# One core, a chunked linear-attention scan and a routed MLP: the loads around the triangular inverses put in another order

## The chip, the cores and the metric

The kernel runs on one core of one Trainium2 chip. A core has five engines that run their own instruction queues side by side: TensorE (PE, with weight loads shown apart as PEld), VectorE (DVE), ScalarE (ACT), GpSimd (POOL) and SyncE (SP). SP computes nothing here; it issues most of the transfers (DMAs), one after the other, and each transfer is carried by the same 16 DMA engines. Every engine takes its instructions strictly in the order in which the program lists them, so an instruction that waits holds up all that is behind it on the same engine. The metric is the device time of the whole kernel in microseconds, the median of some runs.

## What is computed

The reference has two parts. The first is a recurrence over 768 time steps for 4 batches of 8 heads with 40 channels each:

```python
for t in range(S):
    y[:, :, t] = np.einsum('bhd,bhde->bhe', rt, state)
    Sa = np.einsum('bhde,bhe->bhd', state, at)
    state_decay = state * wt[:, :, None, :] - np.einsum('bhd,bhe->bhde', Sa, bt)
    state = state_decay + np.einsum('bhd,bhe->bhde', vt, kt)
```

The second part takes the 3072 rows of y (320 wide) as tokens of a mixture of 8 experts. Each token goes to the expert with the largest logit; an expert keeps the 80 tokens with the largest gate weight and drops the others; each kept token runs through `relu(x @ w1[e]) @ w2[e]` times its gate weight, and every other row of the output is zero.

## The kernel before

**Chunks and units.** The recurrence is cut into 12 chunks of 64 steps. A unit `n` is one chunk of one pair of batches, so there are 24 units (`NU`), and the main loop runs n = 0 to 25. Within a chunk the dependence of the steps on each other is a triangular system for each head. It is solved with inverses of its 32 x 32 diagonal blocks. The blocks of four units (`NG = 4`) are inverted together, one block on each of the 128 partitions, so there are six inversions k = 0 to 5, and inversion k serves units 4k to 4k+3.

**The state's loop.** Unit n needs the state that unit n-2 leaves (two pairs of batches take turns). The path goes: `summed` writes the state on DVE (line 528), POOL copies it (`own_apart`, line 223), PE multiplies it in (`right`, line 447), ACT copies the sum, PE applies the first diagonal inverses (`diagonal(n, 0)`, line 460), then `below` (line 471), then `diagonal(n, 1)`, and `summed(o)` of the unit before, o = n-1, ends the unit with 32 products (line 525). In the same unit the decays and the system of a unit eight ahead, m = n+8, and the scaled keys of m+1 are made (`inverted`, line 326, on DVE, from the keys and b's in `raw_s`; `operand` turns them on PE, line 247).

**The inversion's round trip.** An inversion goes through memory twice:

- `system_kept(m)` writes a unit's blocks to the DRAM tensor `blocks` (line 353).
- `fetch(k)` reads the blocks of four units into the tile `lt` (line 365; 4 transfers of 128 KB, on SP). `lt` and `tt` have one buffer each.
- `begin(k)` masks `lt` into `tt` on POOL (line 370).
- `step(k, i)`, i = 1 to 30, are two DVE instructions each (lines 381 and 384) that work on `lt` and `tt`.
- `end(k)` writes `tt` to `solved` (line 387), and `returned(k)` reads it back into `dt` in another layout (line 394; 4 transfers of 128 KB), from where `diagonal` takes it.

**The order of the work.** The order on each engine is written out by hand: `do(f)` chains the instructions of each call behind the ones before, engine by engine. So the order of calls in the loop is the order of every queue, SP's included. Inversion k = n/4 + 1 begins in the unit with n % 4 = 0 (called the opening unit below: n = 0, 4, 8, 12, 16), and its 30 steps are spread over that unit and the three that follow. `pause(steps, us)` takes steps from the list until their estimated costs use up `us`; with 100 it takes all that are left. Once the list is empty, `end` is called, and `returned` a little later.

In the fourth unit of a group the calls that matter here stand in this order: the last steps, `end`, `load(m + 2, "s")` (keys and b's, 4 transfers of 80 KB), `returned` (4), `turned_r` with the load of the next r (2), `fetch` of the next inversion (4), and after these, in `summed` and in the next unit, the loads of v, w and a (2 each) and the unit's own `blocks` (2). All are on SP from the middle of the prelude on (`queues[1] = nc.sync`).

**Lists and experts.** While the last units run, and after them, DVE finds the 80 best gate values per expert by rounds of `max` and `match_replace` (lines 577 and 578), then the kept tokens' numbers are counted out: a threshold is put on all partitions by PE (line 956), two products give counts and positions (lines 966 and 969), a scan and some DVE work give each token's slot, and 24 products with one-hot tiles `hot` (line 985) give the lists of token numbers. `keep_at_work(pool, tag, times)` issues `times` products of zeros of 128 x 256 in bf16 on PE (line 143), whose result nobody reads. Then the experts' rows are gathered and multiplied.

Of the kernel before, what the change touches and what calls it, by code (L numbers as in the profile page):

```python
# [18 lines left out]
def kernel(  # L19
# [42 lines left out]
    NG = 4  # L62
    NCI = NM // NG
# [73 lines left out]
    still = const.tile([128, 256], BF16, name="still")  # L137
    nc.vector.memset(still, 0.0)

    def keep_at_work(pool, tag, times, x=still):  # L140
        p = pool.tile([128, 256], F32, name="still_p", tag=tag)
        for _ in range(times):
            nc.tensor.matmul(p, lhsT=x[:, 0:128], rhs=x, start=True, stop=True)


    with ExitStack() as p1:

        AHEAD = 2 * NG
        NU = NM
# [540 lines left out]
        def do(f, *args):  # L690
            traced = nc.cur_bb.bb.instructions
            at = len(traced)
            f(*args)
            traced = nc.cur_bb.bb.instructions
            for i in traced[at:]:
                if i.engine in kinds:
                    if i.engine in latest:
                        tc.add_manual_dep(i, latest[i.engine], mybir.DependencyInfo(
                            mybir.DependencyClass.NoSync, mybir.DependencyReason.DATA), reason="order")
                    latest[i.engine] = i.name  # L700


        steps, rounds_ = [], []

        def pause(todo, us_):
            while todo and us_ > 0:
                cost, f = todo.pop(0)
                do(f)
                us_ -= cost

        def invert(k):
            steps.extend(((i * (C - 1 - i) * 1.04 + 155) * 2e-3, lambda i=i: step(k, i)) for i in range(1, C - 1))
# [53 lines left out]
        do(operand, NG + 4, False)  # L766
        do(fetch, 1)

        waiting, turn, inverting = [], None, None

        ZEROS = NU - N // zrows
# [2 lines left out]
        for n in range(NU + 2):  # L774
            o, m = n - 1, n + AHEAD
            now, past, coming, next_, begins_ = n < NU, 0 <= o < NU, m < NU, m + 1 < NU, n % NG == 0


            small = []
            if waiting and (n % NG == 0 or not coming):  # L780
                turn, small, then = waiting.pop(0)
            if next_:
                do(decays, m + 1)
            if n == NU - 2:
                do(turned_lists)
            if past:
                do(turned, o)
            if n == NU - 2:
                do(rows_of_lists)
                rounds_.extend(merged)  # L790
            if coming:
                do(system, m)
            if next_:
                do(forward, m + 1)
                do(backward, m + 1)
            pause(small, 1 if coming else 100)
            if next_:
                do(turned_a, m + 1)
            do(together, n, o)
            if past:  # L800
                do(kept_state, o)
            if now:
                do(right, n)
            if coming:
                do(system_kept, m)
            if next_:
                do(doubled, m + 1)
            if now:
                do(right_kept, n)
            if past:  # L810
                do(state_kept, o)
            if begins_ and n + NG < NU:
                inverting = n // NG + 1
                do(begin, inverting)
            pause(steps, 0.7)
            if next_:
                do(decayed_a, m + 1)
            pause(small, 1)
            if begins_ and inverting:
                invert(inverting)  # L820
            pause(steps, 1.6 if begins_ else 0.4)
            if n == NU:
                pause(rounds_, 2)
            back = None
            if inverting and not steps:
                do(end, inverting)
                back, inverting = inverting, None
            if past:
                do(lower, o)
            if coming:  # L830
                do(psi_masked, m)
            if turn and not coming:
                do(turn)
                rounds_.extend(then)
                turn = None

            if next_ and not begins_:
                do(inverted, m + 1)
            if now and begins_:
                do(reads_g, n)  # L840
            if now:
                do(diagonal, n, 0)
            if now and not begins_:
                do(reads_g, n)
            if begins_ and o >= 1:
                do(logits, o - 1)
            if now:
                do(below, n)
            if next_ and begins_:
                do(inverted, m + 1)  # L850
            pause(steps, (2.4, 4.4, 4.4, 100)[n % NG] if coming else (4.5, 6.5, 100, 100)[n % NG])
            pause(rounds_, LISTS.get(n, 0))
            if inverting and not steps:
                do(end, inverting)
                back, inverting = inverting, None
            if next_:
                do(load, m + 2, "s")
            if back:
                do(returned, back)
            if n == NU + 1:  # L860
                do(keep_at_work, ps_t, "t", 14)
            if o >= 1 and not begins_:
                do(logits, o - 1)
            if turn:
                do(turn)
                turn = None
            if now:
                do(turned_r, n)
            if n % NG == NG - 1 and n + 1 + NG < NU:
                do(fetch, (n + 1) // NG + 1)  # L870
            if now:
                do(reads_r, n)
                do(diagonal, n, 1)
                do(beside, n)
            if next_:
                do(operand, m + 1)
            if n == NU:
                do(keep_at_work, ps_t, "t", 12)
            if past:
                do(summed, o)  # L880
            if n == NU:
                do(keep_at_work, ps_t, "t", 10)
            if o >= 1:
                do(rows_out, o - 1)
                do(logits_summed, o - 1)
                i = share_of[o - 1]
                if o - 1 == shares[i][-1]:
                    waiting.append(gate(i))
            if 0 <= n - ZEROS < N // zrows:
                do(fill, n - ZEROS, n)  # L890
# [51 lines left out]
    with ExitStack() as p2:  # L942
        sl = p2.enter_context(tc.tile_pool(name="sl", bufs=1))
        ps_l = p2.enter_context(tc.tile_pool(name="ps_l", bufs=1, space=PSUM))

        keep_at_work(ps_l, "still", 56)
        union = sl.tile([E, cap], F32, name="union")
        nc.vector.tensor_tensor(out=union, in0=lists[0][0:E, 0:cap], in1=lists[1][0:E, 0:cap][:, ::-1], op=Alu.max)  # L950
        thr = sl.tile([E, 1], F32, name="thr")
# [15 lines left out]

        pos = ps_l.tile([128, NSEL], F32, name="pos")
        nc.tensor.matmul(pos, lhsT=behind_b, rhs=selm, start=True, stop=True)
        at = sl.tile([128, NSEL], F32, name="at")  # L970
        nc.vector.tensor_tensor_scan(at, seg, tot, 0.0, op0=Alu.mult, op1=Alu.add)
        nc.vector.scalar_tensor_tensor(out=at, in0=at, scalar=1.0, in1=pos, op0=Alu.add, op1=Alu.add)
# [127 lines left out]
```

## Time and profile before

| what | us |
|---|---|
| median of 3 runs | 600.25 (597.84 to 607.77) |
| the profiled execution, its own time | 595.1 |
| its span, first to last instruction | 593.4 |
| PE busy in the span | 474.4 (80%) |
| DVE busy in the span | 384.1 (65%) |
| ACT, POOL busy | 219.0, 186.8 |
| mean granted TensorE clock | 0.889 |

The profile is of one execution. Busy shares are means over stages of different kinds: the recurrence fills the span up to about 478 us, the lists lie between about 478 and 511 us, the experts after that. For each instruction the trace has its start, its duration, the idle time of its engine before it and what ended that idle time. The granted clock is the share of full speed that TensorE's throttle allows.

### The profile page before, as it was taken

How to read it: one execution, taken by the hardware profiler on the slowest of the kernel's cores; microseconds unless marked ns; L12 is line 12 of the kernel's file. 1: busy time of each engine (PE TensorE's matmuls, PEld its weight loads, DVE VectorE, ACT ScalarE, POOL GpSimd, SP SyncE). 2: the span in 40 equal slices, each digit the busy share in tenths (PEclk: the TensorE clock that was granted, in tenths of full speed). 3: DMA queues.
4: the chain of work that ended last, by engine and by line, in shares of the span. 5: the costliest groups of instructions: out<-in, count | busy, mean ns of one | idle time of the engine just before them, and what ended most of it. 6: DMA issues, size and time to landing. Idle time of an engine off the chain costs nothing. (4 is left out here: it accounts for less than half of the span.)

```text
span 593.4 us, 25360 instructions
## 1 busy us (share of the span) xinstructions
PE 474.4 (80%) x11254; PEld 404.6 (68%) x11254; DVE 384.1 (65%) x871; ACT 219.0 (37%) x416; POOL 186.8 (31%) x277
## 2 busy tenths in 40 slices
PE   3876328599949999599968998698989835999996
PEld 2665317488848888488857887587878724877774
DVE  8766972699738994699748973988468988001010
ACT  1332114265534565266543655254545300010100
POOL 5243111234534442444532444142323210311011
PEclk9977558599968999699987999698999967999999
DMA  4679438554665548565575437236533239899100
GB/s 78 117 148 136 79 86 130 94 109 76 133 103 104 104 89 156 99 108 102 116 125 99 79 91 111 65 71 138 103 72 92 59 96 359 282 372 362 43 15 14
DMA packets 245249, 71.45 MB, mean 120 GB/s; under 512 B 229524, under 2 KB 237972, under 8 KB 245140
## 3 DMA queue, kind: packets, MB, share of 16 engines
q1 hardware_dynamic: 215136, 61.80, 47.6%
q10 hardware_dynamic: 29236, 6.41, 5.7%
q8 instruction: 88, 1.44, 1.0%
q0 software_dynamic: 768, 1.64, 0.9%
q14 instruction: 21, 0.17, 0.1%
HBM read 51.69 MB, written 18.12 MB: 118 GB/s over the span
## 5 line engine op out<-in xcount | busy, mean ns | idle before, releaser
L381 DVE TENSOR_TENSOR tmp<-tt,lt 128x30 f32<-128x30 f32 (+9 forms) x180 | 75.1, 417 | 45.6 <-POOL tt L370 41.1
L384 DVE TENSOR_TENSOR tt<-tt,tmp 128x30 f32<-128x30 f32 (+9 forms) x180 | 88.8, 493 | 6.6
L265 POOL TENSOR_SCALAR_AFFINE_SELECT side<-side 64x1024 f32<-64x1024 f32 x46 | 53.0, 1152 | 48.5 <-ACT side L511 47.0
L247 PE MATMUL tp<-ident,scaled 64*128 64x64 f32 x384 | 21.8, 262 | 40.7 <-DVE scaled L326 37.8
L223 POOL COPY apart<-state 64x320 f32<-64x320 f32 x44 | 20.1, 457 | 107.4 <-DVE state L528 102.0
L525 PE MATMUL yp<-side,scaled 128*64 128x128 f32 (+1 forms) x768 | 50.8, 290 | 2.5 <-POOL side L265 1.9
L1053 DVE TENSOR_SCALAR y<-yp,weight 80x320 f32<-80x320 f32 x8 | 4.4, 547 | 70.1 <-PE yp L1051 70.1
L265 POOL TENSOR_SCALAR_AFFINE_SELECT nt<-nt 64x512 f32<-64x512 f32 x48 | 32.4, 674 | 55.0 <-ACT nt L350 52.7
L247 PEld LDWEIGHTS tp<-ident,scaled 64*128 64x128 f32 x384 | 17.6, 167 | 44.4 <-issue 30.7
L525 PEld LDWEIGHTS yp<-side,scaled 128*64 128x64 f32 x768 | 44.8, 148 | 4.4 <-POOL side L265 2.0
L291 DVE TENSOR_TENSOR_SCAN pt<-decay,begins 128x520 f32<-128x520 f32 x24 | 34.5, 1437 | 13.7 <-ACT decay L285 12.4
L350 ACT COPY nt<-sp 128x1024 f32<-128x1024 f32 x24 | 24.3, 1011 | 47.4 <-DVE ends L296 29.5
L1045 ACT ACTIVATE hT<-hp 128x320 f32<-128x320 f32 x16 | 6.1, 434 | 92.5 <-PE hp L1041 92.5
L460 PE MATMUL pr<-yy,dt 32*32 32x40 f32 x1536 | 37.6, 200 | 0.1
L1051 PE MATMUL yp<-w,hT 128*80 128x320 f32 x128 | 37.4, 439 | 0.0
L418 PE MATMUL yp<-rT,gT 64*64 64x64 f32 x768 | 28.6, 225 | 10.1 <-DVE xT L534 8.6
L312 POOL COPY qd<-qt 128x1024 f32<-128x1024 f32 x24 | 25.0, 1042 | 36.2 <-DVE qt L298 26.5
L460 PEld LDWEIGHTS pr<-yy,dt 32*32 32x32 f32 x1536 | 31.5, 109 | 6.5 <-issue 3.7
L324 PE MATMUL pp<-ident,qd 64*128 64x64 f32 x384 | 21.5, 261 | 17.6 <-POOL qd L312 10.9
L418 PEld LDWEIGHTS yp<-rT,gT 64*64 64x64 f32 x768 | 25.5, 138 | 11.0 <-issue 9.0
L492 ACT COPY vuT<-tp 128x512 f32<-128x512 f32 x48 | 25.8, 589 | 18.2 <-PE tp L247 17.6
L528 DVE TENSOR_TENSOR state<-yp,pt 128x320 f32<-128x320 f32 x22 | 10.7, 487 | 33.2 <-PE yp L525 33.1
(309 smaller groups left out, 1062.9 us busy)
## 6 DMA issues: line engine op xcount, KB each, us to landing
w<-in_moe_w_dram SPq DMA_DIRECT2D x8, 1280.0 KB, 13.3
w<-in_moe_w_dram SPq DMA_DIRECT2D x8, 1024.0 KB, 14.8
blocks<-nt SPq DMA_DIRECT2D x48, 128.0 KB, 3.1
raw_w<-in_w_dram SPq DMA_DIRECT2D x48, 80.0 KB, 3.3
raw_s<-in_b_dram SPq DMA_DIRECT2D x48, 80.0 KB, 3.3
raw_r<-in_r_dram SPq DMA_DIRECT2D x48, 80.0 KB, 3.0
side<-in_v_dram SPq DMA_DIRECT2D x48, 80.0 KB, 2.8
x_rows<-xb ACTq DMA_DIRECT2D x48, 80.0 KB, 2.8
```

What stands on the lines that cost most here:

```text
L247: nc.tensor.transpose(p[:, z, g, :], t[m, z, 2 * g : 2 * g + 2, :].rearrange("p q d -> p (q d)"), ident[m, m])
L265: nc.gpsimd.affine_select(out=o, in_=o, compare_op=Alu.is_gt, fill=0.0, base=0, pattern=[[0, o.shape[1]], [1, T]], channel_multiplier=-1)
L291: nc.vector.tensor_tensor_scan(flat(pt), flat(chunks(n)), flat(begins), 0.0, op0=Alu.mult, op1=Alu.add)
L312: nc.gpsimd.tensor_copy(qd.rearrange("p g z i t -> p (g z) i t"), of[n].pop("qt")[:, :, :, 1:].rearrange("p g z t -> p (g z) t").unsqueeze ...
L350: nc.scalar.copy(nt.rearrange("p z (q g) t -> p q z (g t)", q=2), p.rearrange("p q z g t -> p q z (g t)"))
L381: nc.vector.tensor_tensor(out=tm, in0=t3[:, 0:i, i : i + 1].to_broadcast([128, i, n]), in1=l3[:, i : i + 1, i + 1 :].to_broadcast([128, i, ...
L384: nc.vector.tensor_tensor(out=t3[:, 0:i, i + 1 :], in0=t3[:, 0:i, i + 1 :], in1=tm, op=Alu.add)
L418: yield lambda z=z, g=g, m=m: nc.tensor.matmul(y[m, z, g, 0:T], lhsT=o["gT"][m, z, g, :], rhs=o["rT"][m, g, halves[z]], start=g == 0, stop ...
L460: nc.tensor.matmul(o["pr"][m, h, :], lhsT=dt_[m, (n % NG) * 2 * G + of_head(n, h), :], rhs=o["yy"][m, h, :], start=h == 0, stop=True, skip ...
L492: nc.scalar.copy(vuT[:, :, :, m], p)
L525: nc.tensor.matmul(o["y"][m, z, g, 0 : T if last else T + HB], lhsT=o["s"][:, z, 2 * g + q, :], rhs=x, start=False, stop=True, skip_group_ ...
L1051: nc.tensor.matmul(yp, lhsT=hT[:, f, :], rhs=w2[:, f, :], start=f == 0, stop=f == FK - 1)
```

## The change

Four things are edited.

1. A helper `ended(k)` calls `end(k)` and right behind it `fetch(k + 1)`, if there is such an inversion. The old call of `fetch` behind `turned_r` is gone. So on SP the four reads of the next inversion's blocks stand directly behind the write of the inverses.
2. `returned` and `load(m + 2, "s")` change places: the keys and b's are now requested behind the reading back of the inverses.
3. The steps are spread a little differently. In the opening unit the first pause takes 0.6 instead of 1.6, the small pause of the other units 0.6 instead of 0.4, and the longer pauses of the second and third unit 4.6 instead of 4.4. The early `end` is only allowed in the fourth unit.
4. `keep_at_work` before the lists issues 60 products instead of 56, and a new call issues 26 between the product for the positions (line 969) and the one-hot products.

```diff
+        def ended(k):
+
+            do(end, k)
+            if k + 1 < NCI:
+                do(fetch, k + 1)
+            return k
...
-            pause(steps, 1.6 if begins_ else 0.4)
+            pause(steps, 0.6)
...
-            if inverting and not steps:
-                do(end, inverting)
-                back, inverting = inverting, None
+            if inverting and not steps and n % NG == NG - 1:
+                back, inverting = ended(inverting), None
...
-            pause(steps, (2.4, 4.4, 4.4, 100)[n % NG] if coming else (4.5, 6.5, 100, 100)[n % NG])
+            pause(steps, (2.4, 4.6, 4.6, 100)[n % NG] if coming else (4.5, 6.5, 100, 100)[n % NG])
             pause(rounds_, LISTS.get(n, 0))
             if inverting and not steps:
-                do(end, inverting)
-                back, inverting = inverting, None
+                back, inverting = ended(inverting), None
+            if back:
+                do(returned, back)
             if next_:
                 do(load, m + 2, "s")
-            if back:
-                do(returned, back)
...
-            if n % NG == NG - 1 and n + 1 + NG < NU:
-                do(fetch, (n + 1) // NG + 1)
...
-        keep_at_work(ps_l, "still", 56)
+        keep_at_work(ps_l, "still", 60)
...
         nc.tensor.matmul(pos, lhsT=behind_b, rhs=selm, start=True, stop=True)
+        keep_at_work(ps_l, "still", 26)
```

## The prediction

> **What bounds the kernel now.** I read the waits first, then the queue of SP, then DVE and PE around one of the waits, then the clock. The view of waits names the pair that bears on this change:
>
> ```profile
> DVE tmp L381 <- POOL tt L370: 41.1, 6, 9.1
> POOL tt L370 <- DMA lt<-blocks: 33.1, 5, 8.0
> ```
>
> The columns are total us, number of times, longest. Six times DVE stands before the first step of an inversion until POOL has masked `lt`; five times POOL itself waits for the transfer of `lt`. One per inversion, so each is an event of an opening unit. Why `lt` is late is seen in SP's timeline at the end of the first group (n = 7, then n = 8; columns: start, us, what):
>
> ```profile
> 154.61 0.35 SPq L387 DMA_DIRECT2D solved<-tt  x1
> 155.01 0.81 SPq L201 DMA_DIRECT2D raw_s<-in_k_dram  x1
> 155.87 1.58 SPq L201 DMA_DIRECT2D raw_s<-in_b_dram  x2
> 157.50 0.66 SPq L201 DMA_DIRECT2D raw_s<-in_k_dram  x1
> 158.27 3.70 SPq L394 DMA_DIRECT2D dt<-solved  x4
> 162.40 1.30 SPq L201 DMA_DIRECT2D raw_r<-in_r_dram  x2
> 163.80 3.36 SPq L365 DMA_DIRECT2D lt<-blocks  x4
> 167.26 2.57 SPq L201 DMA_DIRECT2D side<-in_v_dram  x2
> ```
>
> SP issues without a pause from 154.6 on; `lt` is asked for at 163.8, 9.2 us after the last step, because ten transfers stand before it. Nothing else delays it: `lt` was free and `blocks` written by 154.6. DVE and PE then show what the wait costs (idle time and its releaser in brackets):
>
> ```profile
> 172.42 0.19 DVE L381 TENSOR_TENSOR tmp<-tt,lt 128x30 f32<-128x30 f32 x1 [9.08 <-POOL tt L370]
> 176.99 0.88 DVE L326 TENSOR_TENSOR scaled<-raw_s,pp 128x320 f32<-128x320 f32 x2
> ...
> 169.97 1.27 PE L460 MATMUL pr<-yy,dt 32*32 32x40 f32 x32
> 178.01 1.12 PE L247 MATMUL tp<-ident,scaled 64*128 64x64 f32 x16 [6.76 <-DVE scaled L326]
> 179.06 3.33 PE L525 MATMUL yp<-side,scaled 128*64 128x128 f32 x32
> ```
>
> The steps stand before `scaled` on DVE, PE's turning of `scaled` stands before the 32 products that end the unit. So DVE's wait becomes a PE wait of 6.76 us, and it is on the state's path. Last, the view by windows, from one state to the next (us, busy times with counts, then clock, DMA share, GB/s); the first and third rows are opening units, the second an ordinary one:
>
> ```profile
> 157.77:182.51 24.74, 17.04 (x440) 15.26 (x440) 12.25 (x24) 8.74 (x16) 8.17 (x11) 0.72 0.70 112
> 182.51:197.22 14.71, 14.42 (x442) 12.65 (x441) 13.80 (x25) 8.78 (x16) 6.88 (x9) 1.00 0.64 115
> 225.65:250.03 24.38, 16.46 (x440) 14.41 (x440) 14.51 (x34) 9.03 (x18) 8.28 (x12) 0.79 0.72 123
> 293.80:318.79 24.99, 16.57 (x441) 14.49 (x441) 14.51 (x34) 9.12 (x18) 8.27 (x12) 0.80 0.68 118
> 359.88:378.48 18.60, 13.25 (x353) 11.27 (x349) 11.38 (x35) 7.60 (x16) 5.22 (x9) 0.85 0.59 94
> ```
>
> An opening unit takes 10 us more than an ordinary one with as many PE instructions, and the clock is granted at half speed around its gap. Ordinary units are bound by PE (14.42 busy of 14.71) with DVE close behind (13.80).
>
> **Part 1, the fetch moved.** It touches inversions 2 to 5, thus n = 4, 8, 12, 16, with DVE waits of 9.08, 6.55, 7.27 and 6.15 us. Inversion 1 (8.98) is fetched ahead of the loop, unchanged. For n = 4: `solved` is issued at 154.61, the fetch from 155.0 to 158.4 (its 3.36), its last landing is 4.4 after its last issue (median of the page's list of transfers), at 162.2. POOL is free for `begin` at 163.14, so `tt` is ready at 163.14 + 1.27 + 0.15 = 164.6, DVE having arrived at 163.34. The wait falls from 9.1 to about 1.3.
>
> What is late next is PE. Its chain after `below` (end 168.0), with durations of full-clock units (202.8 to 211.4): turning `qd` 0.7, r 0.6, second diagonal 0.7, turning `scaled` 0.65, 32 products 1.95; state at about 172.7. DVE fits beside it: two steps 2.6 (172.42 to 175.0, POOL beside), `scaled` done by 169.9, five steps 3.2, at 173. That is 182.5 - 172.7 = 9.8 before what the moved loads cost. The same working gives 8.8 for n = 8 (250.0 to 241.2), 9.2 for n = 12 (318.8 to 309.6) and 6.6 for n = 16 (378.5 to 371.9; no keys, less clock lost).
>
> **Part 2, what the move pushes back.** `returned` was held by the landing of `solved` (issued 154.61, 158.27 at the first read) and still is: the four fetch issues fill the time that the four key issues filled. So `dt` is asked for within 0.3 us of now in all four groups (solved landed at 157.5, 226.5, 294.2, about 356.1; the fetch would end at 158.4, 226.6, 294.4, 356.3). It lands 0.4 us before its use at n = 4, some 0.6 to 1 before it at n = 8 and 12 (last issue plus the median 4.1), and 3 before it at n = 16. Keys move from 155.0 to about 162.3, landing near 168.6, used at 169: just in time. r moves from 162.4 to 165.6; it lands near 169.7, used at 168.7: about 1.0 late at n = 4, 0.3 and 0.5 at n = 8 and 12, nothing at n = 16, which has no keys to load. v, w and a are issued at the times of now, but the next unit wants them up to 10 us sooner: w lands near 173, wanted at 172.7. I take 0.9 us per group for these three, between nothing and the 2 us by which single issues stretch (0.6 becomes 1.5 to 2.1 in this trace when small packets are queued up).
>
> **A rule against this part.** The Trainium skill (DMA: Bandwidth & Descriptors, Bandwidth) says that transfers under 64 KB are descriptor-dominated and that size sets the efficiency; its table has 1 MB at 6.15 us, thus two 512 KB reads in some 6 us by estimate. The trace's row is nearer: `lt` and `dt` are 4096 packets of 128 bytes each, and in the busiest microseconds the 16 engines took 1400 to 1450 packets, so 8192 need 5.8 us at best and 6.7 at 13 ns each. Both reads in a row thus take what SP needs to issue them (3.4 + 3.7), by the row and by the table. The rule's warning is in the packets: with DMA engines at 0.89 of full use between 155 and 164, `dt` behind 4096 small packets in place of 2048 can land 2048 x 13 ns / 16 = 1.7 us later. By the row this costs PE up to 1.3 at n = 4, 1.1 and 0.7 at n = 12 and 8; since the keys' issues held SP just as long, I take nothing and leave it in the range.
>
> **Part 3, the steps.** Counting the costs in `pause`: 4+4, 8, 9 and 5 steps before, 2+5, 9, 9 and 5 after, in the four units. One step moves from the opening unit into the second. There DVE runs with 0.28 us of gap, and the state follows right behind its last step, so the step (0.78 us at 184 elements) costs 0.7 each for n = 5, 9, 13. For n = 0 and 1 both units hang on DVE and the sum stays. For k = 5 the third unit gets 9 steps in place of 8: 0.8. In all 2.9. Ending early is not reached in the fourth unit (step 30 remains).
>
> **Part 4, products of nothing.** The 56 end at 493.83; the threshold's product starts at 495.55. Four more (0.43) are hidden. The 26 start at 497.5, and the first one-hot product is at 501.50, after four DVE instructions. The clock is granted at 0.50 from 495.9 to 506.2. At half clock (0.21 each: 14 in 486.13 to 489.09) the 26 take 5.5, until 503.0, 1.5 late. At full clock (0.11) they take 2.9 and hide. The Trainium skill (TensorE: Matmul & The Clock Gate, Part 1) says the clock opens after a busy window of about 3.4 us; by it 16 are slow and 10 fast, end at 502.0, 0.5 late. In the row here it opened 2.96 us after the 56 began; by it 14 slow, 12 fast, end 501.8, 0.3 late. PE is already at work from 496.7, and what opens earlier speeds up the one-hot products (now 503.09 to 503.87 for the last eight). Ends: 1.5 lost, 0.5 won. I take nothing.
>
> **The sum.** 9.8 + 8.8 + 9.2 + 6.6 = 34.4; less r 1.8; less v, w, a 2.7; less steps 2.9: **27.0 us saved**. The profiled execution, 595.1 (span 593.4 and 1.7 around it), would take 568.1. It lay 5.15 under the median of the runs shown, 600.25, so the forecast for a median is **573**.
>
> **Rivals.**
>
> - *The loads take the wait's place* (20%). Keys, r and w land 3 to 4 us late per group, because SP's queue is full until 173 and its issues stretch. For it: SP never pauses there, and 162.3 plus 3.3 leaves 0.4 us. Against it: all transfers of a unit need some 9 us of SP in 14.7. Saving 27 - 4 x 3.5 = 13: 587.
> - *The clock gives more* (7%). No PE gap over 3 us is left, opening units fall to 14.7 and nothing lands late: 34.4 - 2.9 + 4 = 36: 564.
> - *The backlog turns it slower* (6%). Eight reads of 1024 small packets in a row stall each issue for as long as the longest in this trace (1.83 for `dt`, 2.1 for `lt`): 15.7 us in place of 7.1. Then `dt`, keys and r are 8.6 us later, each opening unit waits at its first diagonal and again for r at about 177, and the loads of the next unit follow 8.6 later: 4 x (8.6 + 1) = 38 lost against 34.4 - 2.9 won, about 607. It turns at 7.9 us per group. Against it: stretched issues come once in four.
> - The change does as it says: `lt` is free when `end` may go, since both hang on the last step.
>
> **Range and chances.** The forecast has 67%, with 568 to 579 as its own range (r, w, `dt` and the 26 products at their ends). Reaching to the rivals: 561 to 590. About 2% (12 us) can be told from no change, so half of the first rival counts as within it: faster 0.83, within 0.11, slower 0.06.
>
> **What would show it.** Right: `lt` issued within 0.5 us of `solved` for k = 1 to 4; DVE's wait before L381 under 2 us for four inversions and still about 9 for inversion 1; opening units of 15 to 17 us, clock near 1.0 in them; the second units about 0.7 longer. Wrong: a new PE wait on `dt`, r or w of more than 2 us in an opening unit or the one after it; POOL still waiting for `lt`; one-hot products starting after 502 counted from a like start.

## The result, and the profile after

The changed kernel takes **571.62 us** in the median (4 runs, 570.8 to 579.99), the kernel before 599.31 (4 runs). The ratio is **0.9539**, 95% interval 0.9509 to 0.9569: 4.6% faster. The profiled execution went from 595.1 to 570.8 us, its span from 593.4 to 568.8, the mean granted clock from 0.889 to 0.923. The forecast was 573. All ratios in this text leave out the runs that are more than 1.5% above the fastest of their kernel; the profiled executions of `e3_no_products`, `e6_r_on_act_step_back` and `e7_changed_again` are such runs, so these three kernels are judged by the times of the others.

The view of waits of the changed kernel (total us, number of times, longest):

```profile
DVE tmp L381 <- POOL tt L370: 10.2, 2, 9.1
POOL tt L370 <- DMA lt<-blocks: 8.8, 2, 7.1
...
PE tp L238 <- DMA raw_r<-in_r_dram: 2.8, 2, 1.5
```

DVE's wait before the first step is down from 41.1 us in six to 10.2 in two. The 9.1 is inversion 1, whose fetch nobody moved; of the four whose fetch was moved one wait of 1.05 is left. New is the third line: PE waits for r, twice.

SP's timeline at the end of the first group, that is around the end of n = 3 in the count of states, with the opening unit n = 4 behind it (start, us, what):

```profile
152.04 0.35 SPq L387 DMA_DIRECT2D solved<-tt  x1
152.48 4.25 SPq L365 DMA_DIRECT2D lt<-blocks  x4
156.78 4.16 SPq L394 DMA_DIRECT2D dt<-solved  x4
161.01 0.66 SPq L201 DMA_DIRECT2D raw_s<-in_k_dram  x1
161.72 2.24 SPq L201 DMA_DIRECT2D raw_s<-in_b_dram  x2
164.01 0.63 SPq L201 DMA_DIRECT2D raw_s<-in_k_dram  x1
164.74 1.27 SPq L201 DMA_DIRECT2D raw_r<-in_r_dram  x2
166.11 2.29 SPq L201 DMA_DIRECT2D side<-in_v_dram  x2
```

`lt` is asked for 0.44 us behind `solved` (before: 9.2), `dt` 4.7 behind it (before: 3.7), r last of what this unit needs, 12.7 behind (before: 7.8). SP has no pause here, as before. What became of DVE and PE in that unit:

```profile
162.81 0.19 DVE L381 TENSOR_TENSOR tmp<-tt,lt 128x30 f32<-128x30 f32 x1 [1.05 <-POOL tt L370]
167.34 0.88 DVE L326 TENSOR_TENSOR scaled<-raw_s,pp 128x320 f32<-128x320 f32 x2 [3.61 <-PE pp L324]
...
166.60 0.71 PE L324 MATMUL pp<-ident,qd 64*128 64x64 f32 x16
168.79 0.63 PE L238 MATMUL tp<-ident,raw_r 128*128 128x128 f32 x4 [1.48 <-DMA raw_r<-in_r_dram]
169.34 0.76 PE L460 MATMUL pr<-yy,dt 32*32 32x40 f32 x32
```

DVE now waits for PE (3.61) where PE had waited for DVE (6.76), and PE's longest gap is the 1.48 for r. The windows from one state to the next (us, busy times with counts, clock, DMA share, GB/s). In this order: the opening unit n = 4, its successor, n = 8, the fourth unit n = 11, n = 12 and n = 16:

```profile
156.18:172.76 16.58, 14.14 (x440) 12.53 (x440) 9.17 (x22) 8.74 (x16) 8.14 (x11) 1.00 0.77 126
172.76:187.88 15.12, 14.98 (x458) 13.20 (x457) 14.43 (x26) 9.17 (x17) 6.86 (x9) 1.00 0.61 116
218.25:236.34 18.09, 15.87 (x441) 14.03 (x441) 14.18 (x32) 9.03 (x18) 8.32 (x12) 0.91 0.78 131
266.17:284.45 18.28, 16.04 (x420) 14.32 (x413) 10.49 (x19) 8.13 (x15) 6.82 (x9) 0.81 0.74 124
284.45:299.95 15.50, 14.28 (x441) 12.47 (x441) 14.19 (x33) 9.03 (x18) 8.32 (x12) 1.00 0.67 117
341.00:353.30 12.30, 11.40 (x345) 9.92 (x343) 11.29 (x33) 6.53 (x14) 5.37 (x9) 1.00 0.55 92
```

The opening units fell from 24.74, 24.38, 24.99 and 18.60 to 16.58, 18.09, 15.50 and 12.30. Where they got shorter PE did the same number of products in less time: 14.1 to 15.9 us busy in place of 16.5 to 17.0, since the clock stays up (1.00, 0.91 and 1.00 in place of 0.72, 0.79 and 0.80). But the row of n = 11 is a loss: 18.28 for a unit that took 14.06 before. The whole account, from state to state in the two profiled executions (the forecast had v, w and a late for the unit behind the opening one, so their 2.7 stands there):

| units | before | after | saved | predicted |
|---|---|---|---|---|
| opening, n = 4, 8, 12, 16 | 92.7 | 62.5 | 30.2 | 34.4 - 1.8 (r) = 32.6 |
| second, n = 5, 9, 13 | 44.2 | 45.3 | -1.1 | -2.1 (steps) - 2.7 (v, w, a) = -4.8 |
| n = 18 | 13.6 | 14.4 | -0.8 | -0.8 |
| fourth, n = 3, 7, 11 | 41.9 | 49.2 | -7.3 | 0 |
| up to the state of n = 1 | 128.8 | 126.2 | 2.6 | 0 |
| the other units | 132.2 | 131.2 | 1.0 | 0 |
| last state to the end | 140.0 | 140.0 | 0 | 0 |
| sum | 593.4 | 568.8 | 24.6 | 27.0 |

### The profile page after: what moved, and what is told of

Its sections match the earlier page's. It is cut to its first block, busy times and chain, and to the rows that moved or that the text cites. A ratio compares the mean times of both kernels' runs of the same rounds, so it can differ in the third digit from the quotient of the medians.

```text
span 568.8 us, 25418 instructions
## 1 busy us (share of the span) xinstructions
PE 469.9 (83%) x11284; PEld 400.6 (70%) x11284; DVE 382.2 (67%) x871; ACT 219.1 (39%) x416; POOL 188.8 (33%) x277
## 3 DMA queue, kind: packets, MB, share of 16 engines
q8 instruction: 88, 1.44, 1.1%
## 5 line engine op out<-in xcount | busy, mean ns | idle before, releaser
L381 DVE TENSOR_TENSOR tmp<-tt,lt 128x30 f32<-128x30 f32 (+9 forms) x180 | 72.6, 403 | 16.6 <-POOL tt L370 10.2
L525 PE MATMUL yp<-side,scaled 128*64 128x128 f32 (+1 forms) x768 | 48.5, 282 | 0.6 <-DVE side L509 0.6
L525 PEld LDWEIGHTS yp<-side,scaled 128*64 128x64 f32 x768 | 42.9, 144 | 2.4 <-DVE side L509 0.9
L291 DVE TENSOR_TENSOR_SCAN pt<-decay,begins 128x520 f32<-128x520 f32 x24 | 34.2, 1427 | 12.5 <-ACT decay L285 11.1
L460 PEld LDWEIGHTS pr<-yy,dt 32*32 32x32 f32 x1536 | 31.8, 109 | 7.4 <-issue 4.7
L324 PE MATMUL pp<-ident,qd 64*128 64x64 f32 x384 | 20.3, 251 | 17.4 <-POOL qd L312 12.4
L238 PE MATMUL tp<-ident,raw_w 128*128 128x128 f32 x96 | 19.5, 338 | 16.4 <-DMA raw_w<-in_w_dram 14.8
L259 PE MATMUL sp<-rT,vuT 64*64 64x64 f32 x1536 | 30.3, 226 | 3.0 <-ACT nt L350 1.7
```

The costliest lines, as they stand in the source:

```text
L259: nc.tensor.matmul(p[i, q, z, g, :], lhsT=lhs[m, z, g, i], rhs=rhs[m, g, halves[z]], start=True, stop=True)
L291: nc.vector.tensor_tensor_scan(flat(pt), flat(chunks(n)), flat(begins), 0.0, op0=Alu.mult, op1=Alu.add)
L381: nc.vector.tensor_tensor(out=tm, in0=t3[:, 0:i, i : i + 1].to_broadcast([128, i, n]), in1=l3[:, i : i + 1, i + 1 :].to_broadcast([128, i, ...
L460: nc.tensor.matmul(o["pr"][m, h, :], lhsT=dt_[m, (n % NG) * 2 * G + of_head(n, h), :], rhs=o["yy"][m, h, :], start=h == 0, stop=True, skip ...
L525: nc.tensor.matmul(o["y"][m, z, g, 0 : T if last else T + HB], lhsT=o["s"][:, z, 2 * g + q, :], rhs=x, start=False, stop=True, skip_group_ ...
```

## Experiments

Each was timed against the kernel before on the same chip; the ratio is to that. e1 to e4 ran on one chip, e5 to e8 on another, e9 and e10 on a third. Where nothing else is said, the diff is against the changed kernel.

### e1: The fetch moved, the keys left ahead of `returned`

Is the gain from the fetch alone, or does it need the exchange of `returned` and the keys?

```diff
 (against the kernel before)
+        def ended(k):
+            do(end, k)
+            if k + 1 < NCI:
+                do(fetch, k + 1)
+            return k
...
-            if n % NG == NG - 1 and n + 1 + NG < NU:
-                do(fetch, (n + 1) // NG + 1)
```

> The kernel before with one edit: the fetch of the next inversion's blocks right behind the write of the inverses. The keys stay ahead of the reading back of the inverses, the steps and the products of nothing stay as before. Theory (the fetch carries the gain, the new spread of the steps costs in the fourth units): the fetch gives about 31 us less what the order of keys costs; the inverses are now behind fetch and keys, land about 3 us later at n = 4, 8, 12 and hold the first diagonal product by 2 to 3 us each; no cost in the fourth units. About 570 to 575. Rival (fetch and exchange of keys are needed together): the late inverses take half of the gain back, 585 or more.

Measured: 592.78 us, ratio 0.9876 (0.9838 to 0.9914): 1.2% of the 4.6%. Timelines of SP and PE in this kernel, around its first opening unit:

```profile
156.17 0.35 SPq L387 DMA_DIRECT2D solved<-tt  x1
156.61 3.49 SPq L365 DMA_DIRECT2D lt<-blocks  x4
160.15 1.42 SPq L201 DMA_DIRECT2D raw_s<-in_k_dram  x1
161.62 2.43 SPq L201 DMA_DIRECT2D raw_s<-in_b_dram  x2
164.40 0.60 SPq L201 DMA_DIRECT2D raw_s<-in_k_dram  x1
165.07 3.57 SPq L394 DMA_DIRECT2D dt<-solved  x4
...
169.29 0.23 PE L460 MATMUL pr<-yy,dt 32*32 32x40 f32 x2 [2.13 <-DMA dt<-solved]
170.70 1.27 PE L460 MATMUL pr<-yy,dt 32*32 32x40 f32 x30 [1.18 <-DMA dt<-solved]
```

DVE no longer waits here. But `dt` is asked for 8.9 us behind `solved`: four reads of `lt` and four of keys stand between, and the key issues take 4.5 us (1.42 + 2.43 + 0.60). PE stands before its first diagonal for 2.13 and 1.18, and then works at half clock (1.27 for 30 products). The unit's window shows the price:

```profile
159.03:183.19 24.16, 19.84 (x439) 17.39 (x439) 10.72 (x24) 8.74 (x16) 8.13 (x11) 0.72 0.71 120
```

PE is busy 19.84 for the products that take 14.14 in the changed kernel. The three opening units that load keys take 24.16, 25.41 and 23.84: nothing is won. Only n = 16, which has no keys to load, falls, to 13.14. So the wait was removed and another took its place; the theory that the fetch carries the gain fell.

### e8: The exchange alone

```diff
 (against the kernel before)
-            if next_:
-                do(load, m + 2, "s")
             if back:
                 do(returned, back)
+            if next_:
+                do(load, m + 2, "s")
```

> The kernel before with one edit: the reading back of the inverses ahead of the keys, the fetch where it was. Theory (the exchange only lets the fetch go first without making the inverses late; by itself it leaves SP idle until the inverses' write has landed and pushes keys, r and the fetch back by about 3 us): DVE waits about 3 us longer for the fetched blocks in n = 4, 8 and 12, about 605 to 608. Rival (the early inverses are worth something by themselves): 597 or less.

Measured: 607.3 us, ratio 1.0112 (1.0069 to 1.0155): slower, as the theory said. View of waits of this kernel:

```profile
DVE tmp L381 <- POOL tt L370: 46.1, 5, 11.1
...
POOL tt L370 <- DMA lt<-blocks: 41.3, 5, 10.5
```

With the fetch still last the wait before the first step is longer than before (46.1 in place of 41.1), and the opening units take 27.17, 28.54 and 24.80. Alone, one edit brings 1.2% and the other costs 1.1%; together, with the old spread of the steps (e2 below), they bring 4.0%, and the whole change 4.6% (4.4% in its second measurement, e7). **The gain belongs to the pair**: both `lt` and `dt` have to go ahead of the keys, which are needed later.

### e2: The old spread of the steps

```diff
-            pause(steps, 0.6)
+            pause(steps, 1.6 if begins_ else 0.4)
...
-            pause(steps, (2.4, 4.6, 4.6, 100)[n % NG] if coming else (4.5, 6.5, 100, 100)[n % NG])
+            pause(steps, (2.4, 4.4, 4.4, 100)[n % NG] if coming else (4.5, 6.5, 100, 100)[n % NG])
```

> The changed kernel with the steps spread as before (1.6 in the opening unit, 0.4 in the others, 4.4). Theory (from the changed kernel's trace: a step moved ahead of the scaled keys in the fourth unit stalls PE): fourth units n = 3, 7, 11 fall back by 1.1, 2.0 and 4.2 us, second units by 0.3 to 0.4 each and n = 18 by 0.8, n = 0 and 1 lose 2.0 together, and two more steps ahead of the scaled keys cost 0 to 1.5 in each opening unit: some 3 to 7 us faster than the changed kernel, 565 to 569. Rival (the prediction's account: the steps cost 2.9 in all, by DVE time alone): 568.7, with the fourth units unchanged at 15 to 18 us.

Measured: 575.88 us, ratio 0.9599 (0.9557 to 0.9641). That overlaps the changed kernel's 0.9539 (to 0.9569) and its second measurement below, 0.9563: no gain or loss from the spread can be told, and the 3 to 7 us that the theory expected did not come. Its trace shows where they went. The fourth units take 13.87, 13.48 and 14.25, none of the loss of the table above; but its opening units take 18.01, 20.01 and 20.97. The two together are 31.9, 33.5 and 35.2, against 31.8, 33.8 and 33.8 with the changed kernel.

### e3: No products of nothing beyond the old 56

```diff
-        keep_at_work(ps_l, "still", 60)
+        keep_at_work(ps_l, "still", 56)
...
-        keep_at_work(ps_l, "still", 26)
```

> The changed kernel with 56 products of nothing before the lists and none behind the positions. Theory (the products hide and give nothing): the time from the last state to the end stays at 140.0 us, total as the changed kernel, 571.6 within 0.5. Rival (they hold the clock up and gain): the granted clock falls to one half in the list stage and the kernel is 1 us or more slower.

Measured: 578.25 us, ratio 0.9615 (0.9564 to 0.9665), overlapping that of the changed kernel in either measurement. No effect on the time that could be told. The trace agrees: from the threshold's product to the first product with the experts' weights (line 1034 of the kernel before) it is 16.9 us, as before and after the change.

### e4: One step of the fourth unit moved back behind the scaled keys

The table's loss of 7.3 us in the fourth units comes from one step (number 29) that the new small pause takes earlier. The timelines of DVE and PE in n = 11 of the changed kernel:

```profile
274.63 0.66 DVE L381 TENSOR_TENSOR tmp<-tt,lt 128x58 f32<-128x58 f32 x1
275.32 0.67 DVE L384 TENSOR_TENSOR tt<-tt,tmp 128x58 f32<-128x58 f32 x1
275.91 0.87 DVE L326 TENSOR_TENSOR scaled<-raw_s,pp 128x320 f32<-128x320 f32 x2
...
274.14 0.76 PE L471 MATMUL pr<-u,nt 32*32 32x40 f32 x32
276.44 1.59 PE L552 MATMUL xp__5287<-pick,xT 128*128 128x88 f32 x8 [1.54 <-DVE scaled L326]
281.07 3.27 PE L525 MATMUL yp<-side,scaled 128*64 128x128 f32 x32
```

The step stands ahead of `scaled`, and PE's next product was released by `scaled`: 1.54 us of gap in PE (1.70 in n = 3, 1.44 in n = 7; before 0.56, 0 and 0.09). In n = 11 the clock then fell to half: 3.27 us for the 32 products that otherwise take 1.97. The experiment moves this one step back:

```diff
-            pause(steps, 0.6)
+            pause(steps, 0.6 if n % NG != NG - 1 else 0.4)
```

> The changed kernel with the small pause of the fourth unit at 0.4 again, so that step 29 stands behind the scaled keys there as before; all else as changed. Theory (step 29 ahead of the scaled keys holds PE, whose next product waits for a PSUM buffer that the scaled keys free): the PE wait before line 552 in n = 3, 7, 11 falls from 1.4 to 1.7 us to 0.6 or less, these units from 15.2, 15.7 and 18.3 to about 14.1, 14.0 and 14.1, so 7 us faster than the changed kernel, about 564.5. Rival (the fourth units are longer because the fetch and the reading back crowd the queues at their end): they stay at 15 to 18 us and the total at 571.6.

Measured: 578.27 us, ratio 0.9651 (0.9603 to 0.9699): not faster than the changed kernel. Whether it is slower can't be told: the two measurements of that one reach to 0.9569 and 0.9601, but they were not taken beside this one, and e3, which was and has the recurrence of the changed kernel, has 0.9615 (to 0.9665). Windows of this kernel, the first fourth unit and the opening unit behind it:

```profile
142.37:156.65 14.28, 13.94 (x439) 12.31 (x438) 10.88 (x19) 8.78 (x16) 6.76 (x9) 1.00 0.48 102
156.65:176.44 19.79, 16.75 (x440) 14.71 (x440) 9.18 (x23) 8.74 (x16) 8.13 (x11) 0.83 0.85 131
```

The fourth unit is cured (14.28, later 14.10 and 14.35), but the opening unit takes 19.79 in place of 16.58, the next ones 20.48 and 19.56. The state came earlier; `solved` did not, since two steps in place of one now stood behind `scaled`: it was issued 11.4 us into the fourth unit (11.1 in the changed kernel), thus 2.85 us ahead of the next unit's start in place of 4.14. PE got r 13.7 us into the opening unit in place of 12.6, and before that the clock had fallen to half: PE's five groups from the turning of `qd` on took 7.1 us in place of 4.8. So about 1 of the 3.2 us is r, and the rest the clock. Over the kernel PE waits for r three times, 5.7 us in all, in place of twice, 2.8. So **the stall in the fourth unit had hidden a wait for SP's queue**; without it the wait is one unit later. The theory's 7 us did not come.

### e5, e6: r requested on ACT, with and without that step

If SP's queue from `solved` to r is the limit, r on another queue should free it.

```diff
-            load(n + 1, "r")
+        def load_r(n):
+            ...
+                    nc.scalar.dma_start(raw["r"][0][m, :, 0:D], ...)
...
+            if now:
+                do(load_r, n + 1)
```

> The changed kernel with the loads of r issued on ACT at the end of each unit instead of on SP behind the keys. Theory (in a group's last two units the time is set by the queue of SP from the write of the inverses to the load of r; the PE waits for r of 1.4 to 2.8 us at the end of that queue): r lands before PE wants it, its waits vanish, the opening units fall from 16.6, 18.1 and 15.5 to about 15 us: 4 to 6 us faster than the changed kernel. Rival (the 16 DMA engines are full there, so the queue that issues does not matter): r comes as late as before or pushes the inverses back, and the kernel stays within 1.5 us.

> The kernel with r on ACT and also step 29 behind the scaled keys in the fourth unit. Theory (step 29 cost PE 1.4 to 1.7 us in the fourth unit and was hidden by the queue of SP, which gave it back in the opening unit): with r out of that queue the fourth units' 1.0 to 1.5 us are kept, some 3 us under the run with r on ACT alone. Rival (the reading back of the inverses, not r, sets the pair of units): the opening units get longer by as much, no gain over r on ACT alone.

Measured: 584.01 us, 0.9719 (0.9684 to 0.9753), and with the step back 579.35 us, 0.9625 (0.9597 to 0.9653). The first is 1.6% slower than the changed kernel on the same chip. ACT's timeline of the first one, in an ending unit (n = 7):

```profile
219.96 0.64 ACTq L501 DMA_DIRECT2D raw_r<-in_r_dram  x1
220.11 1.07 ACT L340 COPY sT<-tp 128x512 f32<-128x512 f32 x2
220.70 0.64 ACTq L501 DMA_DIRECT2D raw_r<-in_r_dram  x1
221.43 1.82 ACTq L566 DMA_DIRECT2D x_rows<-xb  x2
223.29 0.59 ACT L285 COPY decay<-tp 128x512 f32<-128x512 f32 x1 [2.10 <-PE tp L247]
```

The wait for r is gone, and the opening units take 15.98, 16.75 and 16.45 at full clock. But the issues stand on ACT ahead of `decay`, which comes with a gap of 2.10 (1.16 at this place in the changed kernel) and which DVE's scan of every unit needs: DVE waits for it 18.5 us in 16 times, in place of 11.1 in 7. SP's reads of `lt` stretch (5.04 us for the four at 218.45), and by SP's own waits the read of `dt` now stands 4.3 us in three times for the landing of r. The units behind pay: n = 5, 6 and 13 take 15.93, 18.29 and 16.30 where the changed kernel has 15.1, 14.7 and 15.1. The Trainium skill (DMA: Bandwidth & Descriptors, Issuing engines are not separate DMA queues) says that issuing on several engines only saves time on the sequencer, as all transfers run on the same 16 DMA engines. Here SP's issue time was saved and ACT's spent, and ACT had less of it to spare: that is the reading that fits these waits, not a shown cause of the 1.6%, since the profiled execution (578.07) is the fastest of its six, and why the others take 4 us and more above it is not seen. With r off SP the step back is worth 1% (0.9719 to 0.9625, intervals apart), which fits a step that costs time once the queue no longer hides it.

### e7: The changed kernel again

> The changed kernel once more, beside the others, to see how far its own executions differ. By both theories 571 to 573, with the fourth and opening unit together between 31.5 and 34.5 us.

Measured: 577.47 us, ratio 0.9563 (0.9524 to 0.9601), in agreement with 0.9539. In its profiled execution 10 us were lost behind the last state, but up to there it shows how the same program's units differ. Windows of n = 3, 4 and 11:

```profile
141.86:160.32 18.46, 16.19 (x429) 14.41 (x425) 10.79 (x19) 8.47 (x16) 6.75 (x9) 0.82 0.56 111
160.32:175.94 15.62, 14.13 (x441) 12.64 (x441) 10.04 (x23) 8.73 (x16) 8.12 (x11) 1.00 0.76 131
...
270.14:285.35 15.21, 13.19 (x420) 11.60 (x421) 10.53 (x20) 8.16 (x15) 6.74 (x9) 1.00 0.58 118
```

In the first profile n = 3 kept the clock (15.23) and n = 11 lost it (18.28); here it is the other way round (18.46 and 15.21). The fourth units of `e9_split_fetch`, with the same steps, show the same two kinds (15.32, 18.43 and 18.74). A fourth unit has two lengths: some 15.2 to 15.7, 1.1 and more over before (the step ahead of `scaled`), and some 18.5, with half clock on top.

### e9, e10: The fetch in two parts

The blocks of the first three units are written long before the inverses. They can be read early, if the steps take their row from `tt`, which holds the same numbers, and `lt` is thus free sooner. Then only the fourth unit's part stands between `solved` and `dt`.

```diff
-                do(fetch, k + 1)
+                do(fetch, k + 1, range(NG - 1, NG))
...
+            if n % NG == NG - 1 and n + 1 + NG < NU:
+                do(fetch, (n + 1) // NG + 1, range(NG - 1))
...
-            l3 = inverse[k]["lt"].rearrange("p (s t) -> p s t", s=C)
-            t3 = inverse[k]["tt"].rearrange("p (s t) -> p s t", s=C)
+            l3 = t3 = inverse[k]["tt"].rearrange("p (s t) -> p s t", s=C)
```

> The changed kernel with the fetch in two parts: the blocks of a group's first three units are read in the fourth unit as soon as its own blocks are written (96 KB in each of 4 transfers, 3072 packets), while SP has nothing to issue, and only the last unit's blocks (32 KB in each of 4) behind the write of the inverses. For this the steps read their row from the masked copy instead of the fetched tile, which is the same data, so that the fetched tile is free after the mask. Theory (the queue from the write of the inverses to r, with 8192 small packets in it, sets a group's last two units): the reading back starts when the inverses have landed and is not stretched, r lands some 3 us sooner, and opening units are 15 to 16 us: 3 to 6 us under the changed kernel. Rival (the fetch's place does not matter any more, the reading back is bound by the landing of the inverses): within 2 us of the changed kernel.

The second has the step of the fourth unit back as well:

> The split fetch with step 29 behind the scaled keys in the fourth unit as well. Theory: the queue of SP has room, so the fourth units' shorter time (14 us in place of 15 to 18) is kept: another 2 to 4 us under the split fetch alone, with the pair of units at 29 to 31 us. Rival (the reading back sets the pair whatever the fourth unit does): no gain over the split fetch alone.

Measured: 577.97 us, 0.962 (0.9562 to 0.9678), and 577.73 us, 0.9592 (0.9525 to 0.966). Neither beats the changed kernel. `dt` was not asked for sooner but 5.2 to 6.9 us behind `solved` (3.6 to 5.1 in the changed kernel), though SP had nothing else to issue: in the first of the two kernels, near the end of its second group, it stood from 219.97 to 224.34. The view of SP's own waits of this kernel says for what (L396 is the reading back of `dt`):

```profile
SPq L396 <- DMA x_rows<-xb: 15.0, 6, 4.4
```

For `solved` it waits 5.3 us in all there, in three times. `x_rows` is the write of finished rows of y, issued on ACT; `dt` does not read it. In the first group the wait for `solved` ended 4.1 us behind the write, and `dt` was asked for another 2.5 us later, when the profile has `x_rows` landing. In the changed kernel this wait is 1.0 us in all. Why the split brings it in is not shown; so these two kernels test neither the theory nor its rival, and leave open what an early read of `dt` would be worth.

## Why the prediction was right, point by point

**What bounds the kernel, and Part 1.** Right in place and size. (The line above SP's timeline in the forecast calls its units n = 7 and 8; they are n = 3 and 4, as its sums have it.) For the four opening units the sum had 32.6 us net of r, and 30.2 were measured; the difference is r's, see Part 2. What was to show it did: `lt` 0.43 to 0.44 us behind `solved` for k = 1 to 4, inversion 1's wait still 9.1. The lengths were to be 15 to 17; 16.58 and 15.50 are, 18.09 is not. There PE waited 1.36 us for r and the clock then fell (3.58 us for the 32 products). n = 16 was forecast to save 6.6 and saved 6.3.

**Part 2.** Right in total, with its parts mis-sized. `dt` was to be asked for within 0.3 us of before, counted from `solved`; at n = 4 it was 1.1 later (4.7 and 3.7), as the four issues of `lt` took 4.25 in place of 3.36, and 1.3 later at n = 8; at n = 12 and 16 it was as forecast. So it was no longer the landing of `solved` that held it, as the forecast had it, but the issues of `lt`, behind which it follows at once (their last ends at 156.73, `dt` is asked for at 156.78). It still came in time: the waits show none on it. r, at the end of the same queue, was to be asked for 11.0 behind `solved` and was 12.7 behind. So 1.8 forecast, 2.8 of PE waits measured (1.48 at n = 4, 1.36 at n = 8, none at n = 12), to which the half clock of n = 8 adds 1.6 (3.58 in place of 1.97 for the 32 products): 4.4 in all. v, w and a: 2.7 forecast, but PE waits for none of them around the ends of the three opening units, and n = 5 runs with PE busy 14.98 of 15.12. That these two errors, 2.6 and 2.7, cancel is luck. That `dt`'s coming in time hangs on the place of the keys I had not weighed as a case of its own; with the keys ahead of `dt` the change brings 1.2% instead of 4.6%.

**The rule on small transfers** was rightly set against the row. The two reads in a row took SP 8.4 us at n = 4 (4.25 and 4.16), not the 7.1 of the forecast's row; `dt` came in time all the same. The table of the Trainium skill (DMA: Bandwidth & Descriptors, Bandwidth) is of transfers issued from GpSimd, and these are issued on SP, so its 6 us was a rough estimate from the start. The warning came true where another wait stood close, as in the kernel with the keys ahead of `dt`.

**Part 3** holds the step that failed. The second units lost 1.1 (2.1 forecast) and n = 18 lost 0.8 (0.8 forecast). But the step moved within the fourth unit was costed at nothing; I had counted five steps before and five after and not asked on which side of `scaled` each stands. In the profiled execution it lost 7.3 us: 1.1 to 2 per unit by its place, and 3.1 once by the clock. In the time it is worth much less, as the kernel with the step moved back shows: the opening unit behind it then grows by as much as the fourth one shrinks, or more. What the executions have in common is the pair of the fourth and the opening unit: 38.8, 38.1 and 39.1 us before, 31.8 to 33.8 after, 31.9 to 35.2 with the old steps, 33.9 to 34.6 with the step back, and 31.0 to 34.3 in the changed kernel's second execution. By the timelines the chain is last step, `solved`, then the reads of `lt` and `dt`, the keys and r on SP. With r off that queue (`e5_r_on_act`) the pair is shorter, 30.5 to 31.7, which speaks for it. It is not shown further than that: two executions of one program differ here by as much as the variants do, and with r on ACT the second units are longer.

The total came out close by luck too: the 7.3 us lost in the fourth units, which the sum did not have, met 7.3 that it did not have either (3.7 in the second units, mostly v, w and a, 2.6 at the start and 1.0 in the other units).

**n = 0 and 1** were to keep their sum, and took 2.6 us less. Eight executions with the changed kernel's pauses there reach the state of n = 1 at 126.2 to 128.9 (mean 127.4), four with the old ones at 127.9 to 130.3 (mean 128.9). So some 1.5 us may be the pauses' and the rest is spread; without the 2.6 the profiled execution would have saved 22 rather than 24.6 of the 27.0. The medians of the runs differ by 27.7, so the profiled pair shows somewhat less than the typical gain.

**Part 4.** Right. From the threshold's product to the end of the last one-hot product it is 7.9 us after and 8.3 before; to the first product with the experts' weights it is 16.9 in both; in the changed kernel the turning of the rows ahead of it waits for their gather (0.61). Last state to end: 140.0 in both.

**The rivals.** "The loads take the wait's place" happened in part: r was late by 1.4 us in two groups, not all loads by 3 to 4 in every group. In the half of the change without the exchange it is what happened, though on `dt`. "The backlog turns it slower" did not come: the eight reads took 8.4 us in place of the 15.7 it needs.

## What to carry to other kernels

On a queue that issues without a pause, moving one transfer forward pushes back all it passes: list what is needed first, and order the queue by that. Here the two reads ahead of the keys gained 4.0 to 4.6%, either half alone 1.2% or less than nothing. When an engine's stall is taken out and the time doesn't move, look at the next unit before blaming the measurement: add up the units that share one chain, not single ones.

## What the hardware showed that I had not expected

- **Where a gap of PE lies in time counts for the clock, not its length alone.** In the fourth units gaps in PE of 1.19, 1.44 and 1.70 us left it at full speed, 1.54, 1.94 and 2.13 did not (over two executions); in the opening units 1.48 did and 1.36 did not. In every trace of this case the granted clock changes only on a grid of 3.41 us, whose place differs from one execution to the next. The Trainium skill (TensorE: Matmul & The Clock Gate, Part 1) says that the activity window is free-running, which fits. Windows of that grid in the changed kernel (PE's busy time is the second number after the stretch, the clock the third from the end). The first has the gap of n = 11, the second follows it, the third has the gap of n = 7:

```profile
273.53:276.94 3.41, 1.87 (x59) 1.68 (x56) 3.31 (x7) 1.01 (x2) 2.28 (x3) 1.00 0.02 5
276.94:280.35 3.41, 3.41 (x48) 2.99 (x49) 0.20 (x1) 1.25 (x3) 0.00 (x0) 0.50 0.72 190
212.08:215.49 3.41, 2.15 (x44) 1.97 (x44) 1.90 (x6) 1.29 (x3) 0.70 (x2) 1.00 0.17 66
```

Behind the gap of n = 11 the clock fell, behind that of n = 7 it did not. Of the eight gaps above, the four with PE busy for 2.05 us or less of such a window were followed by half clock, the four with 2.15 or more were not: the 1.48 and the 1.70 lie across a boundary and leave each window 2.3 or more. It is no full rule: in n = 13 of the second execution the clock fell behind a window with 2.35. In n = 11 the products behind the gap took 8.3 us in place of 5.2: the fall cost twice the gap itself.
- **The issue of a transfer is not a constant.** Single reads of `dt`, all of 1024 packets of 128 bytes, held SP for 0.39 to 1.72 us within one group and up to 2.32 in another, while other reads of that kind were queued. A price per issue is a range as soon as small packets are under way.
